# First four pairs of a chunked scan: products over 128 tokens, full-height tiles, and a new order of all pieces

## The chip, the cores and the metric

The kernel runs on one core of a Trainium2 chip. The metric is device microseconds of one execution, and the median of the runs is compared. One execution of each kernel is also profiled; its instructions, waits and transfers are what this text reads. TensorE (PE) multiplies, and its weight loads are listed apart as PEld. VectorE (DVE), ScalarE (ACT) and GpSimd (POOL) do the elementwise work, and SyncE (SP) issues the transfers.

## The reference

Two blocks follow each other. The first is a chunked scan (Mamba-2's SSD) over 4 batches, 8 heads and 768 tokens, with a head width of 32 and a state of 16:

```python
cum = np.cumsum(log_a[chunk])
M = (C @ B.T) * exp(cum[i] - cum[j]) * (i >= j)
y = M @ x + (C @ state) * exp(cum)
state = exp(sum) * state + sum_j exp(cum[-1] - cum[j]) * B[j] x[j]
```

The heads are then laid side by side to 256 channels (`x` below is that `y`), and a mixer follows:

```python
h = xt @ U @ V                      # xt: tokens last; rank 32
u = x + h.transpose(0, 2, 1)
out = u + np.maximum(u @ w_ch1, 0.0) @ w_ch2
```

with `w_ch1` of 256 x 1024 and `w_ch2` of 1024 x 256. U, V and both weights arrive as 64-bit floats and are turned into 32-bit ones on the chip.

## The kernel before, in words

**Pairs.** The scan takes 128 tokens as one block and two blocks as one pair, so there are 12 pairs, three for each batch. A block holds two chunks of 64 tokens. A pair is worked in steps, each named by a letter in the plan:

- `Q`, `P` (`prep`, L471): VectorE scales B and C by the decays F.
- `V`, `T` (`turning`, L483): TensorE transposes them, ScalarE copies the result to T and, masked by head parity, to Cm (a variant lets VectorE do Cm).
- `g` (`gram`, L518): C B^T. One product takes one head pair r (32 rows), one half p (64 columns) and one block c, with 128 moving columns: 16 products, in tiles of 32x64. Results lie in four PSUM banks.
- `m`, `M` (`mask`, L531): VectorE applies the causal mask to two of these banks each, 128x256 an operation, as a bitwise AND.
- `s` (`state`, L548) and `u` (`update`, L563): TensorE forms each chunk's addition to the state, VectorE runs the recurrence, POOL spreads the states by head (`Sm`, L585).
- `i`, `j` (`inter`, L615): C times the carried state, in two parts. Between the parts stands a guard on POOL (`apart`, L590, the copy at L592), which waits for the products before and holds up those behind.
- `n` (`intra`, L642): M x, 32 products, each over 64 rows (half p) and 32 columns, with 64 moving columns.
- `y` (`yout`, L657): ScalarE copies the result of one bank to yT; `t`, `O`, `o` turn it to tokens first (L671).

**Mixer.** For each batch: `p` (L694), `q` (L702) and `a` (L712) form h and add it to u. For batch 0, `U` are plain f32 products with `w_ch1` (L756, by the helper at L740), eight for each half of the tokens, and `d` the products with `w_ch2`. For the other batches the operands are split in parts first (`S`, `f`, `e`, `h`, `J`). All products of the mixer show under L740, all VectorE operations under L162, since a wrapper records them.

**Conversion.** `c` steps (`to_fp32`, L412) convert the weights, a block at a time: c1 is U and V together; c0 and c2 are the two halves of the first quarter of `w_ch1`; c3 to c5 are its other quarters (w1f); c6 to c9 are `w_ch2` (w2c). `R` refines them for the later batches. Work tiles come from a rotating set named words, of 15.

**Order.** Nothing is reordered by the compiler. `LOADS` and then `PLAN`, a string of words executed from left to right (`follow`, L875), fix the order in which every engine gets its instructions; each engine works its own queue in order. `A0`, `A1` (L371) make the decays F out of the logarithms; `K0` (L390) makes the chunk decays kept; `F` words are fills (L141), products of ones that keep TensorE occupied. Loads (`b`, `x`, `W`, `w`, `Z`, `z`, `B`, `X`, `L`) go into SP's queue in the order of the plan.

Of the kernel before, what the change touches and what calls it, by code (L numbers as in the profile page):

```python
# [10 lines left out]
FP32 = mybir.dt.float32  # L11
INT32 = mybir.dt.int32
# [20 lines left out]

LOADS = (
    'b0.0 b0.1 b0.2 x0.0 x0.1 b1.0 b1.1 b1.2 ')
PLAN = (
# [40 lines left out]


@with_exitstack
def kernel(  # L80
# [285 lines left out]
    for v in range(2):  # L366
        half = slice(v * H, v * H + H)
        vector.tensor_scalar(out=causal[half], in0=upto[half, half], scalar1=-1.0,
                                scalar2=None, op0=ALU.mult)

    def decays(bs, tag="w", which=range(2)):  # L371

# [98 lines left out]
    def prep(k, c=0, n=2):  # L471

        b, q = pairs[k]
        if "BC" not in st.setdefault(k, {}):
            st[k]["BC"] = att.tile([P, 2, 2, NH, N], FP32, tag="BC", name="BC", bufs=3)
        for g in [slice(4) if n == 2 else slice(c, c + 1) if c < 2 else slice(2, 4)]:
            part = st[k]["BC"].rearrange("p i c h n -> p (i c) h n")[:, g]
            vector.tensor_tensor(
                out=part, in0=bc_sb[k].rearrange("p h i c n -> p (i c) h n")[:, g],
                in1=F[:, b, q].rearrange("p h i c -> p (i c) h")[:, g, :, None].to_broadcast(  # L480
                    part.shape), op=ALU.mult)
# [32 lines left out]
    def four(tags, *dims):  # L514

        return [bank(tags[r], *dims) for r in range(4)]

    def gram(k, tags="xxzz"):  # L518
        s = st[k]
        s["g"] = g = four(tags, 2, 2, H)  # L520
        for c in range(2):
            for p in range(2):
                for r in range(4):
                    rows, cols = ts(r, Q), ts(p, H)
                    nc.tensor.matmul(  # L525
                        out=g[r][cols, c], lhsT=s["T"][rows, 0, c, cols],
                        rhs=s["Cm"][rows, :, :, ts(2 * c + p, Q)].rearrange("r v t i -> r v i t"),
                        start=(c == 0), stop=True,
                        skip_group_check=True)

    def mask(k, rows=range(4)):  # L531
        s = st[k]
        g = s["g"]
        if "M" not in s:
            s["M"] = att.tile([P, 4, 2, 2, H], FP32, tag="M", name="M")
        M = s["M"]
# [61 lines left out]
    def channels(k):  # L598

        s = st[k]  # L600
        if "y" not in s:
            s["y"] = [bank("y", 2, 2, H) for p in range(2)]
            s["seen"] = set()
        return s["y"]

# [9 lines left out]
    def inter(k, part):  # L615
# [3 lines left out]
        b, q = pairs[k]  # L619
        s = st[k]  # L620
        y = channels(k)
        after = [apart(k)] if part else []
        for c in range(2):
            for r in range(4):
                p = (part + r // 2) % 2
                own = st.get(("Sm", b, 4 * q + 2 * c + p))
                assert own is not None or 4 * q + 2 * c + p == 0
                if own is not None:
                    product = nc.tensor.matmul(  # L629
                        out=y[p][ts(r % 2, H), r // 2, c], lhsT=own[ts(r, Q)],  # L630
                        rhs=s["T"][ts(r, Q), 1, :, ts(2 * c + p, Q)].rearrange("r t i -> r i t"),
                        start=fresh(k, p, range(2 * (r % 2), 2 * (r % 2) + 2)),
                        stop=True, skip_group_check=True)
                    if part == 0:
                        behind.setdefault(k, []).append(product)
                    for op in after:
                        tc.add_manual_dep(
# [4 lines left out]
    def intra(k):  # L642

        s = st[k]
        y = channels(k)
        for n in range(2):
            for c in range(2):
                for p in range(2):
# [8 lines left out]
    def yout(k, p):  # L657
        b, q = pairs[k]
        if b not in yT:
            yT[b] = mix.tile([P, NCB, S], FP32, tag="yT", name="yT")  # L660
            ytok[b] = mix.tile([P, NC, DM], FP32, tag="ytok", name="ytok")
        yp = yT[b][:, :, ts(q, 2 * P)].rearrange("p g (c v i) -> p g c v i", c=2, v=2)
        nc.scalar.copy(out=yp[:, :, :, p], in_=st[k]["y"][p])  # L663

# [260 lines left out]
```

## Time and profile before

| | us |
|---|---|
| median of 3 runs | 220.32 |
| range of the runs | 219.8 to 224.22 |
| the profiled execution | 220.41 |
| its span, first to last instruction | 218.7 |
| TensorE busy | 210.3 |
| weight loads busy | 182.4 |
| VectorE busy | 154.0 |
| ScalarE busy | 114.2 |
| POOL busy | 17.7 |

The profiled execution's time is its span and 1.7 us around it. Matmuls are pipelined, so that a busy TensorE is not one at its peak; the busy time of weight loads separates the stages better. A timeline row has start, length, engine, line, operation, output and inputs, shapes and count, and in brackets the idle time before it and what ended it. A plain f32 product stands as two records.

### The profile page before, as it was taken

The numbers are of one execution on the slowest core, as the hardware profiler recorded it, in microseconds if no ns is written. First come the engines' busy times: TensorE is split into PE (matmuls) and PEld (weight loads), VectorE is DVE, ScalarE is ACT, GpSimd is POOL, SyncE is SP. The second block draws the span as 40 slices with busy tenths as digits, with TensorE's granted clock in tenths as the row PEclk, the third lists the DMA queues.
The fourth block names the chain that finished last, engine by engine and source line by source line (L and its number), as shares of the span: only waits on it lengthen the run. The fifth ranks groups of instructions, "written<-read, shape, count | busy, mean of one in ns | idle before, by whom it ended". The sixth has DMA issues, their size and how long they took to land.

```text
span 218.7 us, 6992 instructions
## 1 busy us (share of the span) xinstructions
PE 210.3 (96%) x2988; PEld 182.4 (83%) x2988; DVE 154.0 (70%) x330; ACT 114.2 (52%) x261; POOL 17.7 (8%) x41
## 2 busy tenths in 40 slices
PE   7999899999899999999999999999999999999993
PEld 4667566665677889998998999999999999999992
DVE  4687689999983996349796697566575945757813
ACT  3335967798357554645555458153565364466220
POOL 6021020010300210002120000100000000000000
PEclk9999999999999999999999999999999999999999
DMA  6986879896082170080000450100000010100003
GB/s 87 132 118 150 152 103 330 233 207 88 3 124 47 19 132 4 18 126 3 27 3 1 53 118 0 51 10 24 0 0 24 17 34 3 48 3 22 3 24 120
DMA packets 69519, 14.56 MB, mean 67 GB/s; under 512 B 63793, under 2 KB 67697, under 8 KB 69489
## 3 DMA queue, kind: packets, MB, share of 16 engines
q1 hardware_dynamic: 69488, 14.13, 32.5%
q8 instruction: 23, 0.38, 0.8%
q14 instruction: 8, 0.06, 0.1%
HBM read 10.98 MB, written 3.15 MB: 65 GB/s over the span
## 4 chain that ended last, share of the span: by engine, by line
PE 83%; DVE 11%; issue 2%; ACT 1%; DMA 1%; POOL 0%; DVEq 0%; POOLq 0%; ACTq 0%
PE x L740 27%; PE z L740 22%; PE y L740 12%; DVE words L162 5%; PE y L651 3%; PE y L629 3%; PE x L525 2%; PE w L671 2%; DVE M L162 2%; PE w L494 2%; DVE S L162 2%; PE w L557 1%; PE z L525 1%; PE w L694 1%; DMA a_sb<-in_a_dram 1%
## 5 line engine op out<-in xcount | busy, mean ns | idle before, releaser
L162 DVE SCALAR_TENSOR_TENSOR words<-words 128x768 fp32r<-128x768 f32 (+6 forms) x44 | 33.8, 799 | 0.3
L740 PE MATMUL x<-u,w 128*128 128x384 f32 x144 | 32.1, 342 | 0.0
L740 PE MATMUL z<-u,w 128*128 128x384 f32 x144 | 32.1, 342 | 0.0
L740 PEld LDWEIGHTS x<-u,w 128*128 128x128 f32 x144 | 24.6, 188 | 0.4 <-issue 0.2
L740 PEld LDWEIGHTS z<-u,w 128*128 128x128 f32 x144 | 24.3, 188 | 0.4 <-issue 0.2
L740 PE MATMUL x<-w2c,words 128*128 128x256 f32 x112 | 22.8, 339 | 0.7 <-DVE w2c L162 0.7
L745 ACT ACTIVATE x<-x 128x384 f32<-128x384 f32 (+1 forms) x30 | 13.6, 454 | 18.8 <-PE x L740 17.3
L745 ACT ACTIVATE z<-z 128x384 f32<-128x384 f32 (+1 forms) x27 | 12.5, 463 | 18.3 <-PE z L740 14.5
L740 PE MATMUL y<-w,words 128*128 128x256 f32 x144 | 20.3, 280 | 0.0
L740 PEld LDWEIGHTS x<-w2c,words 128*128 128x128 f32 x112 | 18.2, 189 | 2.4 <-DVE w2c L162 0.9
L162 DVE SCALAR_TENSOR_TENSOR words<-x,words 128x384 fp32r<-128x384 f32 x24 | 13.0, 552 | 9.7 <-ACT words L774 9.6
L740 PEld LDWEIGHTS y<-w,words 128*128 128x128 f32 x144 | 19.2, 188 | 0.0
L162 DVE SCALAR_TENSOR_TENSOR words<-z,words 128x384 fp32r<-128x384 f32 x24 | 12.8, 550 | 6.7 <-ACT words L774 6.7
L740 PE MATMUL x<-w,words 128*128 128x256 f32 x96 | 14.3, 285 | 0.0
L585 POOL TENSOR_TENSOR Sm<-S,own 128x256 f32<-128x256 f32 (+1 forms) x12 | 8.1, 676 | 76.3 <-DVE S L162 44.7
L774 ACT ACTIVATE words<-x 128x384 fp32r<-128x384 f32 x24 | 11.4, 488 | 5.6 <-PE x L740 5.6
L774 ACT ACTIVATE words<-z 128x384 fp32r<-128x384 f32 x24 | 11.3, 492 | 5.0 <-PE z L740 5.0
L162 DVE SCALAR_TENSOR_TENSOR S<-S,kept,w 128x64 f32<-128x64 f32 x40 | 11.2, 279 | 2.8 <-PE w L557 0.9
L740 PEld LDWEIGHTS x<-w,words 128*128 128x128 f32 x96 | 12.9, 189 | 0.1
L740 PE MATMUL z<-w2c,words 128*128 128x256 f32 x56 | 11.5, 339 | 0.2 <-DVE S L162 0.2
L651 PE MATMUL y<-M,x 64*32 64x64 f32 x768 | 10.5, 225 | 1.0 <-issue 0.9
L663 ACT COPY yT<-y 128x256 f32<-128x256 f32 x24 | 7.8, 380 | 6.9 <-PE y L629 6.9
(154 smaller groups left out, 400.0 us busy)
## 6 DMA issues: line engine op xcount, KB each, us to landing
words<-in_moe_w_ch_dram SPq DMA_DIRECT2D x7, 512.0 KB, 5.2
x<-in_x_dram SPq DMA_DIRECT2D x24, 128.0 KB, 3.4
out_dram<-ytok SPq DMA_DIRECT2D x24, 128.0 KB, 1.7
bc<-in_B_dram SPq DMA_DIRECT2D x24, 64.0 KB, 3.0
bc<-in_C_dram SPq DMA_DIRECT2D x12, 128.0 KB, 3.2
words<-in_moe_w_ch_dram SPq DMA_DIRECT2D x2, 256.0 KB, 3.7
words<-in_moe_V_dram SPq DMA_DIRECT2D x4, 48.0 KB, 1.9
words<-in_moe_U_dram SPq DMA_DIRECT2D x1, 192.0 KB, 4.0
```

The source lines that it names most:

```text
L162: self.last = call(*args, **kwargs)
L494: nc.tensor.transpose(out=tp[:, i, v], in_=s["BC"][:, i, c + v].rearrange("p h n -> p (h n)"), identity=ident)
L525: nc.tensor.matmul(out=g[r][cols, c], lhsT=s["T"][rows, 0, c, cols], rhs=s["Cm"][rows, :, :, ts(2 * c + p, Q)].rearrange("r v t i -> r v i ...
L557: nc.tensor.matmul(out=s["A"][p][ts(r, Q), v], lhsT=s["BC"][half, 0, v, 2 * r:2 * r + 2].rearrange("p h n -> p (h n)"), rhs=x_sb[k][half, ...
L585: nc.gpsimd.tensor_tensor(out=s["Sm"][:, sl], in0=s["S"][:, sl].rearrange("p i (s d) -> p i s d", s=2), in1=own2[:, b, 4 * q:4 * q + sl.st ...
L629: product = nc.tensor.matmul(out=y[p][ts(r % 2, H), r // 2, c], lhsT=own[ts(r, Q)], rhs=s["T"][ts(r, Q), 1, :, ts(2 * c + p, Q)].rearrange ...
L651: product = nc.tensor.matmul(out=y[p][ts(i, Q), n, c], lhsT=x_sb[k][half, c, h], rhs=s["M"][half, h // 2, c, h % 2], start=fresh(k, p, [i] ...
L663: nc.scalar.copy(out=yp[:, :, :, p], in_=st[k]["y"][p])
L671: nc.tensor.transpose(out=t[:, c, g], in_=yT[b][:, g, ts(2 * q + c, P)], identity=ident)
L740: nc.tensor.matmul(out=t, lhsT=lhsT, rhs=rhs, start=start, stop=True, skip_group_check=True)
L745: nc.scalar.activation(t, t, AF.Copy, scale=1.0 + EPS)
L774: nc.scalar.activation(gs[j, m // 2][0][:, m % 2], t, AF.Relu, scale=NEAR)
```

## The change

It applies to the first four pairs (`LIGHT`): the three of batch 0 and the first of batch 1.

- `gram`: one product for a head pair and a block over all 128 tokens, 256 moving columns: 8 products in tiles of 32x128.
- `mask`: the mask is `lower`, with the causal triangle in the two diagonal 64x64 blocks and zero elsewhere, made in the setup on POOL. An operation covers 128x512. Its output goes to two tiles of the words set in place of the M tile.
- `intra`: M x with all 128 rows and 128 moving columns, 16 products in tiles of 128x32.
- `inter`: the bank is chosen by head pair and not by chunk, and the guard on POOL is left out.
- `yout`: the copy writes 256 adjacent elements.
- `prep`: pairs 2 and 3 (`SCALED`) are scaled on POOL and not on VectorE.
- `PLAN`: all pieces and loads of the whole kernel stand in another order. At the beginning, V's loads (`Z0`) stand ahead of pair 2's, K0 and three fills ahead of A0, and pair 1's state behind its masks; pair 4's C B^T stands behind the first plain product. `LOADS` is the same.

```diff
+LIGHT = range(0, 4)
+SCALED = (2, 3)
 PLAN = (
-    'x1.1 F2.0 A0 Q0.1 x1.0 Q0.0 b2.2 A1 F2.1 Q0.2 V0.1.1 V0.0.0 K0 F3.3 Q1.2 Q1.1 g0 m0 Q1.0 s0 '
-    'V1.1.2 M0 n0 u0.0 u0.1 V1.0.2 b3.0 F2.1 Q2.1 s1 u1.0 u1.1 i0 g1 m1 F3.0 M1 b2.0 Q2.0 b2.1 Q2.2 '
...
-    'c0 o2 F2.3 v0 x4.1 b4.1 b4.2 u3.0 u3.1 p0 c2 n3 c0 P4 c0 i3 q0 c2 b5.2 b5.0 T4 T4 j3 y3.0 y3.1 '
-    'W2 W3 b5.1 W4 a0.0 c2 c2 a0.1 x4.0 w5 c3 c3 c3 X5 g4 c4 w8 c3 t3 w6 U0.0.0 m4 c4 U0.0.1 P5 c4 '
...
+    'x1.1 F2.0 Z0 K0 b2.2 F2.3 F2.1 F1.0 A0 A1 Q0.1 b2.1 Q0.0 b2.0 Q1.0 x1.0 x2.0 Q0.2 x2.1 b3.1 '
+    'b3.2 s0 V0.0.0 F2.1 u0.0 u0.1 V0.1.1 F3.3 b3.0 z0 Q1.2 g0 W0 Q2.2 Q2.1 V1.0.2 x3.0 F3.0 Q1.1 '
+    'V1.1.2 Q2.0 x3.1 b4.2 i0 M0 m0 g1 m1 M1 b4.1 n0 V2.1.3 j0 y0.1 b4.0 W2 s1 W1 V2.0.2 y0.0 u1.0 '
+    'n1 s2 W3 W4 u1.1 u2.0 u2.1 w6 g2 b5.1 m2 M2 i1 j1 y1.0 i2 y1.1 O0.0 t1 n2 c1 c1 x4.0 P3 j2 y2.0 '
+    'c1 y2.1 b5.0 w8 c0 T3 T3 O2.1 c0 s3 c1 g3 u3.0 c0 w5 u3.1 o2 m3 p0 i3 v0 M3 c0 P4 q0 n3 j3 c3 '
+    'y3.1 a0.1 T4 T4 a0.0 b5.2 c3 y3.0 c2 U0.1.0 c3 c3 g4 c5 t3 c2 U0.0.0 M4 c2 c5 c5 U0.1.3 c4 X5 '
...
+    lower = const.tile([P, 2, H], INT32)
+    nc.gpsimd.memset(lower, 0)
+    for v in range(2):
+        half = slice(v * H, v * H + H)
+        nc.gpsimd.tensor_copy(out=lower[half, v], in_=causal[half])
...
-            vector.tensor_tensor(
+            (nc.gpsimd if k in SCALED else vector).tensor_tensor(
...
+        if k in LIGHT:
+            s["g"] = g = four(tags, 2, 2, P)
+            for c in range(2):
+                for r in range(4):
+                    nc.tensor.matmul(
+                        out=g[r][:, c], lhsT=s["T"][ts(r, Q), 0, c],
+                        rhs=s["Cm"][ts(r, Q), :, :, ts(c, H)].rearrange("r v t i -> r v i t"),
+                        start=(c == 0), stop=True, skip_group_check=True)
+            return
...
+        if k in LIGHT:
+            t = raw.tile([P, 2 * WCOLS], INT32, tag="words", name="words", bufs=NWORDS)
+            M = t.rearrange("p (r c s i) -> p r c s i", r=2, c=2, s=2)
+            s.setdefault("Ms", {})[rows[0] // 2] = M.bitcast(FP32)
+            for r in rows:
+                vector.tensor_tensor(
+                    out=M[:, r % 2].rearrange("p c s i -> p (c s) i"),
+                    in0=g[r].bitcast(INT32).rearrange("p c s i -> p (c s) i"),
+                    in1=lower.rearrange("p v i -> p (v i)")[:, None, :].to_broadcast([P, 4, P]),
+                    op=ALU.bitwise_and)
+            return
...
-            s["y"] = [bank("y", 2, 2, H) for p in range(2)]
+            s["y"] = [bank("y", 2, P) if k in LIGHT else bank("y", 2, 2, H) for p in range(2)]
...
-        after = [apart(k)] if part else []
+        light = k in LIGHT
+        after = [apart(k)] if part and not light else []
...
+                    at = r // 2 if light else p
                     product = nc.tensor.matmul(
-                        out=y[p][ts(r % 2, H), r // 2, c], lhsT=own[ts(r, Q)],
+                        out=y[at][ts(r % 2, H), c, ts(p, H)] if light else
+                        y[p][ts(r % 2, H), r // 2, c], lhsT=own[ts(r, Q)],
...
+        if k in LIGHT:
+            for n in range(2):
+                for c in range(2):
+                    for i in range(4):
+                        nc.tensor.matmul(
+                            out=y[n][ts(i, Q), c], lhsT=x_sb[k][:, c, 4 * n + i],
+                            rhs=s["Ms"][n][:, i // 2, c, i % 2], start=fresh(k, n, [i]),
+                            stop=True, skip_group_check=True)
+            return
...
+        if k in LIGHT:
+            nc.scalar.copy(out=yT[b][:, p, ts(q, 2 * P)],
+                           in_=st[k]["y"][p].rearrange("p c i -> p (c i)"))
+            return
```

More of the change, by code (lines that the diff above doesn't have):

```diff
@@ L628, in inter @@
                 if own is not None:
+                    at = r // 2 if light else p
                     product = nc.tensor.matmul(
-                        out=y[p][ts(r % 2, H), r // 2, c], lhsT=own[ts(r, Q)],
+                        out=y[at][ts(r % 2, H), c, ts(p, H)] if light else
+                        y[p][ts(r % 2, H), r // 2, c], lhsT=own[ts(r, Q)],
                         rhs=s["T"][ts(r, Q), 1, :, ts(2 * c + p, Q)].rearrange("r t i -> r i t"),
-                        start=fresh(k, p, range(2 * (r % 2), 2 * (r % 2) + 2)),
+                        start=fresh(k, at, range(2 * (r % 2), 2 * (r % 2) + 2)),
                         stop=True, skip_group_check=True)
-                    if part == 0:
+                    if part == 0 and not light:
                         behind.setdefault(k, []).append(product)
```

70 rows, old and new, of the table PLAN are left out of this document.

## The prediction, made before the changed kernel ran

> **What bounds the kernel now.** I read the page first: the busy shares, the forty slices, the chain by engine.
>
> ```profile
> PE 210.3 (96%) x2988; PEld 182.4 (83%) x2988; DVE 154.0 (70%) x330; ACT 114.2 (52%) x261; POOL 17.7 (8%) x41
> PEld 4667566665677889998998999999999999999992
> DVE  4687689999983996349796697566575945757813
> PE 83%; DVE 11%; issue 2%; ACT 1%; DMA 1%; POOL 0%; DVEq 0%; POOLq 0%; ACTq 0%
> ```
>
> Over the whole span TensorE bounds. The weight loads (PEld) separate two stages: 4 to 7 tenths in the first twelve slices, 9 from the middle on. VectorE is densest in slices 7 to 12. So I cut the span with the windows view (columns: stretch, its length, then busy time and instructions of PE, PEld, DVE, ACT, POOL, then clock and DMA).
>
> ```profile
> 5.93:33.83 27.90, 25.43 (x716) 17.93 (x720) 21.54 (x65) 15.91 (x46) 4.12 (x9) 1.00 0.83 139
> 34.81:60.00 25.19, 24.48 (x248) 15.54 (x246) 24.34 (x54) 17.88 (x36) 3.49 (x3) 1.00 0.67 158
> 80.00:203.50 123.50, 123.50 (x1520) 118.47 (x1505) 83.38 (x152) 63.50 (x144) 4.67 (x10) 1.00 0.12 28
> ```
>
> From 80 us TensorE is full and does only work that the change leaves alone. What the change can move is how late the full stage begins. Two queues decide that: until 34 us VectorE works 21.54 of 27.90 us (6.36 idle); from 35 to 60 us VectorE is full (24.34 of 25.19) with the weight conversion while TensorE does the plain products of batch 0. The chain in order of time shows both.
>
> ```profile
> 35.08 1.29 PE x L740 x4
> 50.54 2.50 DVE words L162 x4
> 59.30 0.61 DVE w2c L162
> 59.95 1.25 PE x L740 x5
> 65.41 0.87 PE z L740 x4
> ```
>
> The first line is two plain f32 products of 384 columns, in 4 records: 1.29 us, 0.84 ns a column and record. The next three show the conversion on VectorE and TensorE taking up again when the last converted block (w2c) is there, at 59.9. The last is one down piece of batch 0 (four records of 256 columns): 0.87 us.
>
> **Part 1: the products themselves.** Timeline rows:
>
> ```profile
> 28.58 0.86 PE L694 MATMUL x<-ytok,UV 128*32 128x256 f32 x16
> 29.37 0.86 PE L651 MATMUL y<-M,x 64*32 64x64 f32 x64
> 30.16 0.49 PE L629 MATMUL y<-T,Sm 32*64 32x64 f32 x12
> 33.45 0.35 PE L525 MATMUL x<-Cm,T 32*64 32x128 f32 x2 [0.16 <-ACT Cm L504]
> 34.19 0.30 PE L525 MATMUL z<-Cm,T 32*64 32x128 f32 x2
> 34.43 0.66 PE L671 MATMUL w<-ident,yT 128*128 128x128 f32 x4
> 34.92 0.49 PE L740 MATMUL x<-yT,w1f 128*128 128x384 f32 x1
> ```
>
> M x for a pair is 64 records of 64 columns, 29.37 to 30.16: 0.79 us. One after another at 0.84 ns they would take 3.44 us, so 4.4 of 8 tiles run at a time. After, it is 32 records of 128 columns: again 3.44 us in a row, in four tiles. The nearest row with 128x32 tiles is the projection L694: 8 records of 256 and 8 of 128 columns, 2.58 us in a row, took 0.79 (28.58 to 29.37), 3.3 at a time. So 0.86 (four at a time) to 1.05 us. C B^T is 32 records of 128 columns now (first and last quoted, 0.74 us of starts in that pair), 16 of 256 after: the same 0.86 to 1.05. TensorE pays 0.2 to 0.6 us more a pair, 0.7 to 2.3 us for four. All of it lies before 34 us, where TensorE waits for VectorE; I count none there, except that masks begin later after C B^T (0.35 us, for two of four, below). Uncovered, it is the 2.3 us. The guard on POOL between the two inter-chunk halves (L592) goes for four pairs. Its row stands in the next fence: 0.487 us each, and the waits shown are POOL's own. I count nothing, and put a gain of at most 4 x 0.49 us into the range. The copies to yT keep their 256 elements: nothing.
>
> **Part 2: VectorE up to the first plain product.** Groups by form (busy, mean ns of one):
>
> ```profile
> L162 DVE TENSOR_TENSOR M<-x,causal 128x256 int32<-128x256 int32 x24 | 9.0, 417 | 0.6 <-PE z L525 0.5
> L162 DVE TENSOR_TENSOR yT<-x,yT 128x384 f32<-128x384 f32 x8 | 4.4, 552 | 2.4 <-PE x L712 2.4
> L162 DVE TENSOR_TENSOR BC<-bc,F 128x512 f32<-128x512 f32 x9 | 6.2, 684 | 0.5 <-issue 0.5
> L162 DVE TENSOR_TENSOR BC<-bc,F 128x128 f32<-128x128 f32 x6 | 1.6, 285 | 1.0 <-ACT F L386 1.0
> L162 DVE TENSOR_TENSOR BC<-bc,F 128x256 f32<-128x256 f32 x3 | 1.3, 421 | 0.4 <-ACT F L386 0.4
> L162 DVE TENSOR_SCALAR words<-words 128x256 int32<-128x256 int32 x4 | 1.4, 396 | 0.0
> L162 DVE TENSOR_SCALAR words<-words 128x512 int32<-128x512 int32 x14 | 6.1, 476 | 0.0
> L585 POOL TENSOR_TENSOR Sm<-S,own 128x256 f32<-128x256 f32 x8 | 6.0, 745 | 40.1 <-DVE S L162 36.0 <-PE z L740 4.1
> L592 POOL COPY settled<-slot 128x1 f32<-128x1 f32 x12 | 5.8, 487 | 48.7 <-PE y L629 37.5 <-PE y L651 11.1
> ```
>
> Sixteen masks grow from 256 to 512 elements. 256 to 384 elements is 417 to 552 ns, so 512 is about 0.683: 16 x 0.266 = +4.26 us. The scalings of pairs 2 and 3 go to POOL: 2 x 0.285 + 0.421 + 0.684 = -1.67. Reordering puts two conversion steps of 256 behind (-0.79) and two of 512 ahead (+0.95); the two operations of the chunk decays (below) leave this stretch, -1.05. Counted in the program's order, the operations from the first scaling to the additions that release the first plain product sum to 24.65 us of durations before and 26.26 after. Before, 24.65 occupied 21.54 us, so 26.26 occupies 23.0: +1.5 us.
>
> **Part 3: the start.** K0 (chunk decays, L394, L397) and three fills (L141) now stand ahead of A0 (L379) in TensorE's queue.
>
> ```profile
> 4.64 0.87 PE L379 MATMUL w<-la,ref 128*128 128x192 f32 x2
> 7.75 0.49 PE L394 MATMUL z<-la,middle 128*128 128x192 f32 x2
> 8.62 0.81 PE L141 MATMUL y<-one 128*128 128x384 f32 x2
> 12.84 0.60 PE L141 MATMUL x<-one 128*128 128x256 f32 x2
> 5.93 0.49 DVE L162 TENSOR_TENSOR BC<-bc,F 128x128 f32<-128x128 f32 x2 [1.02 <-ACT F L386]
> 6.78 0.42 DVE L162 TENSOR_TENSOR BC<-bc,F 128x256 f32<-128x256 f32 x1 [0.36 <-ACT F L386]
> 7.73 0.61 DVE L162 TENSOR_SCALAR Cm<-w,slot 128x128 f32<-128x128 f32 x2 [0.53 <-PE w L494]
> 8.82 0.53 DVE L162 TENSOR_TENSOR words<-z,mine 128x352 f32<-128x352 f32 x1 [0.48 <-PE z L397]
> 9.38 0.52 DVE L162 TENSOR_REDUCE kept<-words 128x44 f32<-128x352 f32 x1
> 23.65 0.63 DVE L162 TENSOR_SCALAR words<-words 128x384 int32<-128x384 int32 x2 [1.21 <-DMA words<-in_moe_U_dram]
> ```
>
> K0 took 0.87 us of starts (7.75 to 8.62). The fills are 640 columns in two records, 1.08 us at 0.84 ns. That is 2.0 us, and up to 3.9 if records run half as fast, as L379 does near 4.6 us (0.87 for two of 192 columns). I take 2.9, in between, as the array warms on the way. VectorE's first scaling goes from 5.93 to 8.8. VectorE does the decays in that wait. Of its 6.36 us of idle time the first pieces (0.36, 0.53, 0.48) then have no cause, and neither has the 1.21 us for U, whose load stays at about the same place in SP's queue while its conversion comes later; twice 0.35 us come with the longer C B^T: 4.5 us. The V loads now stand ahead of pair 2's loads and of half of x of pair 1 on SP; pair 1's state is also needed later, so nothing, and the range covers 1 us. POOL's scaling of pair 3 has 512 elements, 1.4 us at 745 ns for 256, against 0.68 on VectorE; masked by VectorE's queue, in the range too.
>
> **The sum.** 8.8 + 23.0 + 4.5 = 36.3 us for the additions that ended at 33.83 (33.28 and 0.55 long): +2.5 us. Before, C B^T of pair 4 and transposes stood ahead of the first plain product (33.45 to 34.92); now behind it, and the waits inside go, which leaves TensorE 2.8 us later at equal work. From there to 60 us TensorE idled 0.7 us (25.19 - 24.48), which its larger backlog fills. The profiled execution took 220.41 us (span 218.7, 1.7 around it; the median of the runs, 220.32, is the same within 0.1). 220.4 + 2.8 - 0.7 = 222.5 us.
>
> The Trainium skill, "TensorEngine Tiling (Array Packing)", Key Properties, says that changing the tiling mode drains TensorE. C B^T and the inter-chunk product shared one shape and no longer do. An estimate by that rule: two more switches in each of four pairs, each one record's 0.22 us, is 1.8 us, which would make 224.3; the row L629 starts 0.79 us after L651 and does not separate a drain, so no run here shows it yet.
>
> **Rivals.** (a) *Slower: conversion decides.* From those additions to the last converted block VectorE has 29.3 us of durations before and 31.9 after. Before it took 26.1 us (33.8 to 59.9), so after 28.4, ending at 64.7. TensorE has about 30 us of work ahead of the first product that needs the block (15 plain products at 1.29, four down pieces at 0.87, some 7.5 us of C B^T, M x, states and transposes of pairs 4 to 6), which lasts to about 66.5. For it: the cover is thin, and the chain ran on VectorE until 59.9. If the cover is not there because those products wait for masks and earlier blocks, the whole lateness of the conversion, 64.7 - 59.9 = 4.8 us, counts: 225.2. It decides as soon as VectorE loses 2 us more than counted. (b) *Shorter chain.* Four independent pairs, states first and no guard, leave VectorE 1 us of idle time instead of 4.5, and the start costs 2.0: 222.5 - 3.5 - 0.9 = 218.1, with the guard's 2 us also gained 216. Against it: nothing shows the guard on the path. (c) *The tiles do not overlap four at a time:* 3.44 us instead of 0.86 for 8 products, +20 us, of which at most 6 are covered: over 230; L694 speaks against it. (d) *Issue bounds the products.* If M x's 64 records were bound by their number, half of them would halve 0.79 us, for C B^T likewise: 3 us less, 219.5. The Trainium skill, "TensorE: Matmul & The Clock Gate", section "Wait — 56ns, not 53.3ns?", states a floor of about 25 ns from start to start. The trace disagrees: 64 records in 0.79 us are 12 ns apart.
>
> **How the numbers follow.** Chances: forecast 0.54, (a) 0.18, (b) 0.22, (c) 0.03, (d) 0.03. The forecast's own range is 220 to 224.5. 2% of 220.4 is 4.4 us, about what a measurement of this kernel can tell from no change: below 216.0 faster, above 224.8 slower. Faster: half of (b), 0.11. Slower: (a) and (c), 0.21. Within: 0.68. The range runs from (b) without the guard, less half a microsecond of lost idle time in the late stage, to (a) with 1.8 us of the uncounted product cost of 2.3: 217.5 to 227.0.
>
> **What would show it.** First scaling at 8.8 us, not 6; masks of 512 elements at 0.68 us; M x and C B^T of a pair at 0.9 to 1.05 us; the additions done at 36.3; the last w2c at 64.7 with no TensorE wait for it. A first scaling before 7.5, or a TensorE wait of 2 us or more near 60, makes the forecast wrong, on either side.

## The result and the profile after

The changed kernel takes 221.72 us in the median of 9 runs (221.42 to 222.71), the kernel before 220.56 on the same chip (219.12 to 224.22). The ratio is 1.0078, 95% interval 1.0054 to 1.0102: slower by 0.8%, or 1.2 to 2.2 us, and within the 2% that the text before calls no change. The profiled executions are 221.42 and 220.41 us, 1.0 apart. (One kernel below, the order alone, was disturbed in four of its six executions, the profiled one among them; its ratio rests on the other two, 227.1 and 228.0 us.)

The page of the changed kernel, busy shares and the chain by engine:

```profile
PE 211.9 (96%) x2796; PEld 182.4 (83%) x2796; DVE 155.9 (71%) x326; ACT 114.0 (52%) x261; POOL 17.5 (8%) x44
PE 88%; DVE 5%; ACT 3%; issue 1%; DMA 1%; DVEq 0%; ACTq 0%
```

VectorE's share of the chain fell from 11% to 5%, TensorE's rose from 83% to 88%: the kernel is a little slower although the wait at the conversion is gone. The stretches, cut at the first scaling, the additions and 60 us (length, then busy time of PE, PEld, DVE, ACT, POOL, clock, DMA):

```profile
7.78:35.40 27.62, 24.72 (x495) 16.58 (x494) 23.27 (x59) 14.31 (x42) 4.89 (x9) 1.00 0.91 184
35.40:60.00 24.60, 24.36 (x287) 15.01 (x286) 23.74 (x56) 20.68 (x42) 1.60 (x3) 1.00 0.60 120
60.00:80.00 20.00, 20.00 (x422) 16.21 (x422) 10.77 (x28) 8.23 (x19) 1.60 (x4) 1.00 0.50 78
```

VectorE works 23.27 of 27.62 us up to the additions; from 35.40 on TensorE is idle for 0.24 us and from 60 to 80 us not at all. The rows that answer the predicted steps, the start and VectorE's first (the masks as groups, with mean ns), then TensorE's:

```profile
4.68 0.72 PE L401 MATMUL z<-la,middle 128*128 128x192 f32 x2
6.88 0.49 PE L386 MATMUL w<-la,ref 128*128 128x192 f32 x2
7.78 1.03 DVE L164 TENSOR_TENSOR BC<-bc,F 128x128 f32<-128x128 f32 x4 [0.72 <-ACT F L393]
L164 DVE TENSOR_TENSOR words<-x,lower 128x512 int32<-128x512 int32 x8 | 5.1, 685 | 1.8 <-PE z L531 1.7
L164 DVE TENSOR_TENSOR words<-z,lower 128x512 int32<-128x512 int32 x8 | 5.1, 683 | 0.9 <-PE z L531 0.9
34.85 0.55 DVE L164 TENSOR_TENSOR yT<-z,yT 128x384 f32<-128x384 f32 x1
64.53 0.69 DVE L164 SCALAR_TENSOR_TENSOR w2c<-words 128x512 f32<-128x512 f32 x1
...
10.77 0.53 PE L531 MATMUL x<-Cm,T 32*128 32x256 f32 x2 [0.27 <-DVE Cm L164]
11.70 0.44 PE L531 MATMUL z<-Cm,T 32*128 32x256 f32 x2
12.07 0.44 PE L501 MATMUL x<-ident,BC 128*128 128x128 f32 x2
18.21 1.08 PE L680 MATMUL y<-words,x 128*32 128x128 f32 x32
19.27 0.32 PE L584 MATMUL w<-x,BC 64*32 64x64 f32 x8
34.99 1.56 PE L783 MATMUL x<-yT,w1f 128*128 128x384 f32 x4
```

K0 begins at 4.68, A0 at 6.88, and the first scaling is at 7.78. Masks take 0.68 us each, and what VectorE waits for ahead of them is C B^T (1.7 and 0.9 us). C B^T of the first pair lasts 1.30 us from its first start to the next product's (10.77 to 12.07), M x 1.06 (18.21 to 19.27). The additions end at 35.40, against 33.83 before. The last w2c is converted at 64.53 to 65.22, and no row of TensorE waits for it.

### The profile page after: what moved, and what is told of

Read it like the earlier page. It is cut to its first block, busy times and chain, and to the rows that moved or that the text cites. A ratio compares the mean times of both kernels' runs of the same rounds, so it can differ in the third digit from the quotient of the medians.

```text
span 219.7 us, 6607 instructions
## 1 busy us (share of the span) xinstructions
PE 211.9 (96%) x2796; PEld 182.4 (83%) x2796; DVE 155.9 (71%) x326; ACT 114.0 (52%) x261; POOL 17.5 (8%) x44
## 4 chain that ended last, share of the span: by engine, by line
PE 88%; DVE 5%; ACT 3%; issue 1%; DMA 1%; DVEq 0%; ACTq 0%
PE x L783 31%; PE z L783 23%; PE y L783 12%; PE y L658 3%; PE y L690 2%; PE w L501 2%; PE x L531 2%; PE w L714 2%; DVE words L164 2%; PE x L541 1%; PE w L584 1%; DVE S L164 1%; PE w L737 1%; ACT Cm L511 1%; PE z L541 1%
## 5 line engine op out<-in xcount | busy, mean ns | idle before, releaser
L783 PEld LDWEIGHTS z<-u,w 128*128 128x128 f32 x144 | 24.8, 188 | 0.1
L783 PE MATMUL y<-w,words 128*128 128x256 f32 x144 | 19.5, 280 | 0.0
L783 PEld LDWEIGHTS y<-w,words 128*128 128x128 f32 x144 | 18.5, 188 | 0.2 <-ACT z L788 0.2
L783 PE MATMUL x<-w,words 128*128 128x256 f32 x96 | 13.7, 282 | 0.0
L783 PE MATMUL x<-yT,w1f 128*128 128x384 f32 x32 | 11.4, 489 | 0.0
L505 ACT COPY T<-w 128x512 f32<-128x512 f32 (+1 forms) x10 | 5.7, 568 | 10.3 <-PE w L501 10.3
```

Source lines behind the costliest of these rows:

```text
L505: nc.scalar.copy(out=s["T"][:, :, c:c + n], in_=tp)
L783: nc.tensor.matmul(out=t, lhsT=lhsT, rhs=rhs, start=start, stop=True, skip_group_check=True)
```

## The experiments

Prices are stated against the kernel before, as ratios with intervals; 0.1% is 0.22 us. The changed kernel's own ratio, 1.0078, is what most of them are held against.

**1. The order alone.** `LIGHT` and `SCALED` empty, so that only `PLAN` differs from before in the pairs.

```diff
-LIGHT = range(0, 4)
-SCALED = (2, 3)
+LIGHT = range(0)
+SCALED = ()
```

> The order of after with the products, masks, copies and scalings of before for all twelve pairs. Theory (VectorE's stretch up to the additions sets the end; the large masks and the late start are what the new order has to make up for): sixteen masks are 0.266 us shorter (-4.26), two pairs' scalings come back to VectorE (+1.67), so the additions come about 2.6 us earlier than 35.4, near 33, and the time is 221.7 - 2.6 = 219.1, or 1.0 more where C B^T for 64 columns does not help: 218.5 to 220. Rival A (the order of the loads and late pieces is what costs the 1.2 us, products and masks lie under other work): no change against after, 221.7. Rival B (the new order only fits independent products; the guard and the dependent halves stall in it): slower than after, 222.5 to 224.

Measured: ratio 1.0335 (1.0281 to 1.0389), 7.4 us slower than before. The theory had it at 219, and it fails: without the large masks this kernel is slower than both, and beyond rival B's 224 too. VectorE's rows, from the stretch of 5.88 to 16.12 us, in which the granted clock of its profiled execution was 1.0:

```profile
13.46 0.83 DVE L164 TENSOR_TENSOR BC<-bc,F 128x256 f32<-128x256 f32 x3 [1.94 <-DMA bc<-in_C_dram]
14.97 0.29 DVE L164 TENSOR_TENSOR BC<-bc,F 128x128 f32<-128x128 f32 x1 [0.69 <-DMA bc<-in_B_dram]
```

Two scalings of pair 2, at the head of VectorE's queue, wait 1.94 and 0.69 us for loads of C and B, and everything behind them waits too. That is a part of the 7.4 us; experiment 7 finds another.

**2. The products alone.** The new products, masks and copies in the order of before, all scalings on VectorE; the guard of the light pairs is left out here too.

```diff
-SCALED = (2, 3)
+SCALED = ()
-PLAN = ( ... the new order
+PLAN = ( ... the order of before
```

> The order of before with the light products, masks and copies for the first four pairs, all scalings on VectorE. Theory: VectorE gets 4.26 us more before the additions, nothing is taken off it, the guard is gone, C B^T takes 1.3 us a pair and not 0.74; of VectorE's 6.36 us of idle time in that stretch at most about 1.5 can take it up: 220.5 + 3 to 5 = 223.5 to 225.5, first plain product at 38 to 40 us. Rival A (masks lie in VectorE's idle time, the order costs): 220.5 to 221.5. Rival B (the guard and the two-part products were on the path and make up for the masks): below 220.5.

Measured: 226.76 us, ratio 1.0301 (1.0267 to 1.0334). The additions end at 39.66:

```profile
39.11 0.55 DVE L164 TENSOR_TENSOR yT<-z,yT 128x384 f32<-128x384 f32 x1
```

That is 5.8 us later than before, of which the sixteen masks are 4.26. This fits the theory in kind, with the masks on the path, and the time is about 1.3 us above its range. Two other things are in it. TensorE stops for 0.88 us at 154.69, a kind of stop that experiment 7 finds. And the granted clock of this execution was 0.5 from 32.50 to 35.91 us, which is in the 5.8; three executions at a clock of 1.0 took 226.58 to 227.51 us all the same. So either half of the change measures 3% slower, and both together 0.8%.

**3. The scalings back on VectorE.**

```diff
-SCALED = (2, 3)
+SCALED = ()
```

> After, with the scalings of pairs 2 and 3 on VectorE again. Theory (VectorE before the additions is the path): +1.67 us there less what its remaining 4.3 us of idle time takes up, so 222.3 to 223.4, additions done at 36 to 37. Rival (POOL's slower scalings were late for their pairs, so the move bought nothing): 221.0 to 221.9.

Measured: 223.72 us, ratio 1.0167 (1.0131 to 1.0203), 0.9% or 2.0 us above the changed kernel. Two rows of VectorE, and POOL's scaling of 512 elements in the changed kernel:

```profile
13.28 1.03 DVE L164 TENSOR_TENSOR BC<-bc,F 128x256 f32<-128x256 f32 x4 [1.99 <-DMA bc<-in_C_dram]
37.04 0.55 DVE L164 TENSOR_TENSOR yT<-z,yT 128x384 f32<-128x384 f32 x1
```

```profile
L485 POOL TENSOR_TENSOR BC<-bc,F 128x512 f32<-128x512 f32 x1 | 1.1, 1107 | 0.0
```

The additions end at 37.59, 2.2 us later. It is not only the 1.67 us of work: the scaling of pair 2 waits 1.99 us for its load, ahead of the masks in the same queue. On POOL a wait for a load holds up nothing on VectorE, though 512 elements take 1.1 us there. A part of the 2.0 is the clock: in the profiled execution it was 0.5 from 15.80 to 19.21 us, and the three executions at 0.988 to 0.990 took 224.06 to 224.84 us; the three at 0.996 to 1.0 took 223.11 to 223.37, 1.4 above the changed kernel.

**4. The decays ahead of the chunk decays,** as they stood before.

```diff
-F2.0 Z0 K0 b2.2 F2.3 F2.1 F1.0 A0 A1 Q0.1 b2.1 Q0.0 b2.0 Q1.0 x1.0 x2.0 Q0.2
+F2.0 Z0 A0 b2.2 A1 Q0.1 b2.1 Q0.0 b2.0 Q1.0 x1.0 x2.0 Q0.2 K0 F2.3 F2.1 F1.0
```

> After, with the decays A0 A1 ahead of the chunk decays K0 and of the three fills, and K0's VectorE work behind the first scalings, as it stood before. Nothing is left out. Theory (the late start costs what it delays): first scaling at 5.9 instead of 7.78 (-1.85), the two operations for the chunk decays come back into the stretch (+1.05), pieces of idle time too: 221.7 - 0.8 = 220.9, additions at 34.6. Rival A (the start has slack because transfers or TensorE set the additions): unchanged, 221.7, with VectorE idle longer further down. Rival B (early fills and K0 are needed for what follows): slower, 222.5.

Measured: 222.35 us, ratio 1.0103 (1.0071 to 1.0135): no gain, and rather 0.5 us more than the changed kernel, though the intervals overlap.

```profile
5.92 0.49 DVE L164 TENSOR_TENSOR BC<-bc,F 128x128 f32<-128x128 f32 x2 [1.09 <-ACT F L393]
7.70 0.63 DVE L164 TENSOR_TENSOR BC<-bc,F 128x128 f32<-128x128 f32 x2 [1.28 <-DMA bc<-in_B_dram]
8.24 0.52 DVE L164 TENSOR_TENSOR words<-z,mine 128x352 f32<-128x352 f32 x1
35.31 0.55 DVE L164 TENSOR_TENSOR yT<-z,yT 128x384 f32<-128x384 f32 x1
```

The first scaling is back at 5.92, but the third, of pair 1, waits until 7.70 for its load of B. In the changed kernel VectorE does the chunk decays in that time, and here they come behind (8.24 to 9.31): the additions end at 35.86, 0.46 later. The late start was nearly free, and undoing it is not.

**5. Without the three fills** ahead of A0.

```diff
-K0 b2.2 F2.3 F2.1 F1.0 A0 A1
+K0 b2.2 A0 A1
```

> After without the three fills between the chunk decays K0 and the decays A0. Only products of ones are left out. Theory (a late start costs little, because pair 1's B lands at 7.7 and its scaling is third in VectorE's queue): first scaling at 6.7 instead of 7.78, third at 7.7 instead of 8.19, so 0.4 to 0.5 us less: 221.3. Rival A (the fills' 1.08 us count in full): 220.7. Rival B (the fills keep the array ready, the first products become slower): 221.7 or more.

Measured: 221.78 us, ratio 1.0105 (1.0067 to 1.0143): nothing gained. ScalarE's and VectorE's rows:

```profile
7.18 0.24 ACT L413 ACTIVATE kept<-kept 128x44 f32<-128x44 f32 x1 [2.69 <-DVE kept L164]
7.32 0.55 ACT L393 ACTIVATE F<-w 128x192 f32<-128x192 f32 x2
7.68 0.37 DVE L164 TENSOR_TENSOR BC<-bc,F 128x128 f32<-128x128 f32 x1 [0.53 <-ACT F L393]
```

A0 is 1 us earlier, and the first scaling still at 7.68. ScalarE works its queue in order, and K0's exponential (L413) stands ahead of that of the decays F (L393): it waits for VectorE's reduction, which ends at 7.14. So the fills were covered, and neither the prediction nor the expectation had looked at ScalarE's queue.

**6. The guard put back** for the light pairs.

```diff
-after = [apart(k)] if part and not light else []
+after = [apart(k)] if part else []
-if part == 0 and not light:
+if part == 0:
```

> After, with the guard on POOL between the two inter-chunk halves put back for the four light pairs. Theory (it lies beside other work, as the prediction counted): 221.7, at most 0.3 more. Rival (its 0.49 us a pair and the wait for M x lie on the path): 222.7 to 223.7.

Measured: 223.50 us, ratio 1.0181 (1.0134 to 1.0227), 1.0% or 2.3 us above the changed kernel. The time is the rival's, but not all of it is shown to be the guard's. The profiled execution was the longest of six (224.79): its first scaling came 0.6 later, its granted clock was 0.5 from 23.47 to 26.88 us (0.83 from 20 to 30), and TensorE stopped for 0.75 us at 57.47, inside one group of M x, as in experiment 7. Its rows around the guard:

```profile
23.37 0.87 PE L658 MATMUL y<-T,Sm 32*64 32x64 f32 x24 [0.41 <-POOL settled L619]
24.06 0.65 ACT L702 COPY yT<-y 128x256 f32<-128x256 f32 x2 [2.92 <-PE y L658]
27.48 1.06 DVE L164 SCALAR_TENSOR_TENSOR words<-words 128x384 f32<-128x384 f32 x2 [2.15 <-ACT words L437]
```

TensorE waits 0.41 us for the guard, ScalarE copies that pair's result at 24.06 instead of 22.69 (0.6 of it from the start), and the conversion of U and V behind that copy keeps VectorE idle for 2.15 us (0.52 in the changed kernel). Of that increase about 0.9 us goes with the clock: the two groups of transposes ahead of the conversion take 1.90 us of starts here and 1.03 in the changed kernel. At a clock of 1.0 four executions took 221.99 to 223.63, with a middle of 223.3, 1.6 above the changed kernel, or 2.1 when each is held against the kernel before that ran beside it. How much of that is the guard and how much a stop like the one at 57.47 isn't separated; the wait of 0.41 us is what is seen of the guard itself.

**7. The order alone, with POOL's scalings:** experiment 1 with `SCALED = (2, 3)`.

> The order of after with the products, masks and copies of before for all pairs, but the scalings of pairs 2 and 3 on POOL as in after. Theory (the order alone lost because scalings that wait for loads stood in VectorE's queue): the waits of 1.9 and 0.7 us for the loads of B and C and 1.67 us of scalings go, which gives 227.1 - 4.3 = 222.8, and the smaller masks bring it below after, 219.5 to 221. Rival (the new order stalls on the guard and on the dependent halves of the old products): 224 to 227, and waits of VectorE for the states and of TensorE around the guard stay.

Measured: 227.27 us, ratio 1.0319 (1.0263 to 1.0375). Up to the additions the theory is right: no load is waited for, and they end at 34.82, 0.6 before the changed kernel's. Then the time is lost again, in places that no one had counted: TensorE stops at 104.28, 146.44 and 156.72 us for 1.33, 1.04 and 0.76 us, and at 18.36, ahead of the additions, for 0.99. A row of each kind, the second from the kernel before (it has one such piece, at 22.59):

```profile
103.95 0.33 PE L584 MATMUL w<-x,BC 64*32 64x64 f32 x11
105.61 0.42 PE L584 MATMUL w<-x,BC 64*32 64x64 f32 x21 [1.33 <-issue]
```

```profile
22.05 0.54 PE L651 MATMUL y<-M,x 64*32 64x64 f32 x34
23.50 0.45 PE L651 MATMUL y<-M,x 64*32 64x64 f32 x30 [0.91 <-issue]
```

In both, TensorE stands still in the middle of one group of equal products, and the releaser is "issue": it waits for nothing that the profile shows. The four pieces are 4.12 us against 0.91 in the kernel before, 3.2 of the 4.4 us between the two profiled executions (224.79 and 220.41).

**8. C B^T in 32x64 tiles,** each product of the light pairs split in two column halves.

```diff
-for r in range(4):
-    nc.tensor.matmul(out=g[r][:, c], lhsT=s["T"][ts(r, Q), 0, c],
+for p in range(2):
+    for r in range(4):
+        nc.tensor.matmul(out=g[r][ts(p, H), c], lhsT=s["T"][ts(r, Q), 0, c, ts(p, H)],
```

> After, with C B^T of the light pairs in tiles of 32x64, eight at a time: each product is split in two column halves, the same multiplications and the same results, 32 records of 256 columns instead of 16. Theory (four tiles of 32x128 start a group only every 0.27 us because the next weights load late; the 0.55 us more per pair are on the path through the masks): with eight tiles 0.9 to 1.0 us a pair and not 1.3, three waits of VectorE 0.3 shorter: 220.7 to 221.2. Rival (the pace is set by the moving data of a row group, which two column halves do not share): twice the records take 1.7 us or more, 222.5 to 223.5.

Measured: 227.62 us, ratio 1.0366 (1.0316 to 1.0417), and both reasons given for it are wrong. VectorE does not see the edit: the additions end at 35.50, 0.10 later. C B^T takes what it took:

```profile
10.80 0.48 PE L532 MATMUL x<-Cm,T 32*64 32x256 f32 x2 [0.27 <-DVE Cm L164]
11.09 0.47 PE L532 MATMUL x<-Cm,T 32*64 32x256 f32 x2
12.07 0.44 PE L501 MATMUL x<-ident,BC 128*128 128x128 f32 x2
...
63.08 0.64 PE L659 MATMUL y<-T,Sm 32*64 32x64 f32 x24 [0.70 <-issue]
106.99 0.41 PE L585 MATMUL w<-x,BC 64*32 64x64 f32 x20 [1.33 <-issue]
149.40 0.29 PE L542 MATMUL x<-Cm,T 32*64 32x128 f32 x1 [1.51 <-issue]
159.38 0.41 PE L784 MATMUL x<-w,words 128*128 128x256 f32 x2 [0.59 <-issue]
```

Eight tiles start a group of eight every 0.27 to 0.29 us, as four started a group of four: 1.27 us for the pair, against 1.30. The loss is the last four rows: 0.70 + 1.33 + 1.51 + 0.59 = 4.13 us of "issue", long after the light pairs are done. With the 0.10 that is 4.2 of the 5.1 us between the two profiled executions.

A theory for these pieces: the page lists a queue named instruction.

```profile
q8 instruction: 22, 0.36, 0.7%
```

22 transfers, in the trace 16,384 bytes each, go with 2796 products and as many weight loads: 5592 / 22 = 254 to a transfer, 64 bytes each. In the trace of the split tiles one begins at 104.79 and ends at 105.75, and TensorE goes on at 106.99; for the others it begins at 60.62, 146.52 and 157.02. Each time TensorE goes on 2.2 to 2.9 us after the transfer's start. In the changed kernel one begins at 104.50, and from 105.8 on TensorE is in products of 384 columns, which need few instructions. So it should matter where in the stream of small products a transfer's boundary falls, and any change in the number of TensorE's instructions moves all later boundaries. Three kernels put that to the test.

**9. The changed kernel, shifted.** Nothing of its work is changed; 32 tiny products replace two thirds of the first fill, in the time in which TensorE waits for its first input.

```diff
-warm(3, "x")
+small = bank("x", 4 * P)
+idle(small, 1)
+for i in range(32):
+    part = slice(i % 4 * Q, i % 4 * Q + Q)
+    nc.tensor.matmul(out=small[part, P + 8 * i:P + 8 * i + 8],
+                     lhsT=one[part].to_broadcast([Q, Q]), rhs=one[part].to_broadcast([Q, 8]), ...
```

> After, with 32 tiny products (32x32 tiles, 8 columns) in place of two thirds of the very first fill, in the time in which TensorE waits for its first input. Everything behind them is unchanged; they only shift TensorE's stream of instructions by 128, counted as two records and two weight loads a product, which is half of one 16 KB transfer of the queue named instruction at 64 bytes each (22 transfers for 5657 records and loads). Theory (where these transfers fall against the dense groups of small products decides the idle pieces put down to issue): the late idle pieces of the version with C B^T in 32x64 tiles, 0.7, 1.3, 1.5 and 0.6 us at about 62, 106, 148 and 159 us, appear here too, though no product of the pairs is changed: 225 to 226.5. Rival (those pieces belong to the products in 32x64 tiles): 221.3 to 222.2, no idle piece.

Measured: 226.85 us, ratio 1.0300 (1.0266 to 1.0334), 2.2% above the changed kernel.

```profile
107.58 0.42 PE L591 MATMUL w<-x,BC 64*32 64x64 f32 x21 [1.29 <-issue]
149.46 0.34 PE L548 MATMUL x<-Cm,T 32*64 32x128 f32 x2 [1.04 <-issue]
159.18 0.62 PE L790 MATMUL x<-w,words 128*128 128x256 f32 x4 [0.49 <-issue]
36.12 0.55 DVE L164 TENSOR_TENSOR yT<-z,yT 128x384 f32<-128x384 f32 x1
PE 87%; DVE 5%; ACT 3%; issue 3%; DMA 1%; DVEq 0%; ACTq 0%
```

Three of the four pieces are there, at the places named, 2.82 us together; "issue" rises from 1% to 3% of the chain. The tiny products also delayed the start: the additions end at 36.67, 1.27 later. With 0.41 us of TensorE's idle time between 60 and 80 us that is 4.5 of the 5.0 us between the profiled executions.

**10. The 32x64 tiles, shifted,** by the same edit.

> The version with C B^T in 32x64 tiles, with the same 32 tiny products ahead. It has 32 products more than after in the light pairs, 128 instructions, so with the tiny ones 256, one whole transfer: theory: the idle pieces at 62, 106, 148 and 159 us go, C B^T takes what it took, 221.7 to 222.5. Rival (they belong to those products): 227 to 228, pieces stay.

Measured: 223.27 us, ratio 1.0136 (1.0110 to 1.0162), 2.3% less than without the tiny products, though they add work. The four pieces are gone, and one of 0.68 us has come at 55.60. The additions end at 36.15, 0.75 later than the changed kernel's; 0.75 + 0.68 is 1.4 of the 1.7 us to its profiled execution. One shift brings the pieces to a kernel that had none, and takes them from one that had four. That they come from TensorE's instruction transfers is shown by these two and by a count over all fourteen traces. Behind 8 us these have 24 pieces of "issue" over 0.25 us on TensorE. Counted among TensorE's records (products, weight loads and the sequencer's own), each of the 24 falls at the same place: 193 records and a multiple of 256 stand ahead of it. Each ends 1.2 to 1.6 us after a transfer has ended. The 0.91 us of the kernel before is one of them.

**11. The order alone with POOL's scalings, shifted,** by the same edit.

> The order alone with scalings on POOL, with the same 32 tiny products ahead. Against after that version has 96 products more, 384 instructions, and with the tiny ones 512, two whole transfers. Theory: the three late idle pieces (1.3, 1.0 and 0.8 us) go, 227.3 - 3.1 = 224.2 or less, down to 222; what stays above after is lost before 35 us in the waits of the old products. Rival: 227, the pieces stay.

Measured: 227.96 us, ratio 1.0328 (1.0294 to 1.0363): the time did not fall. The three late pieces are gone, as expected (after 80 us TensorE is idle for 0.14 us), and others have come early:

```profile
19.37 0.69 PE L697 MATMUL y<-M,x 64*32 64x64 f32 x44 [1.17 <-issue]
22.13 0.48 PE L665 MATMUL y<-T,Sm 32*64 32x64 f32 x11 [0.84 <-POOL settled L626]
24.40 0.90 PE L665 MATMUL y<-T,Sm 32*64 32x64 f32 x20 [1.78 <-issue]
PEclk9999659999999999999999999999999999999999
```

1.17 and 1.78 us of "issue" inside M x and the inter-chunk product, and 0.84 for the guard between them; the additions end at 40.32 instead of 34.82. Not all of these 5.5 us are the stops: the last line, from the page, is the granted clock in 40 slices of 5.65 us, in tenths, and it fell to 0.5 from 23.94 to 34.18 us, right behind them. Whether the stops brought the clock down was not tested. A further stop of 0.63 us stands at 59.86. So a shift moves the pieces, it does not remove them.

**12. Before, with POOL's scalings** and nothing else of the change.

> Before, with nothing of the change but the scalings of pairs 2 and 3 on POOL. TensorE's order is untouched. Theory (VectorE's work ahead of the additions of batch 0, and ahead of the last converted block, is the path in before): 1.67 us less there, a part of it lost as waits, 220.2 - 0.7 to 1.5 = 218.7 to 219.5, additions near 32.5. Rival (POOL takes 1.1 us for 512 elements and has the guards and the spreading of states to do, so pairs 2 and 3 or their guards come late): 220.2 to 221.5.

Measured: 220.47 us, ratio 1.0013 (0.9984 to 1.0043): no difference. VectorE's rows:

```profile
17.97 0.61 DVE L162 TENSOR_SCALAR Cm<-x,slot 128x128 f32<-128x128 f32 x2 [1.48 <-PE x L494]
20.12 0.92 DVE L162 SCALAR_TENSOR_TENSOR S<-S,kept,w 128x64 f32<-128x64 f32 x3 [1.55 <-POOL settled L592]
25.36 0.76 DVE L162 TENSOR_TENSOR M<-z,causal 128x256 int32<-128x256 int32 x2 [2.05 <-PE z L525]
```

VectorE's 1.67 us went, and waits of 1.48, 1.55 (for the guard) and 2.05 us (for C B^T) stand there (0.64, 0.11 and 0.49 at the same places before). The time is the rival's, but the guard is only the second of these waits. Ahead of the third TensorE stopped for 1.15 us ("issue", 22.94 to 24.09) inside M x, right before that C B^T; the kernel before has its 0.91 there. VectorE's work was not what set these rows. No kernel of this study is faster than the one before.

## Why the prediction came out, point by point

*The sum.* Predicted 222.5 us, the forecast of a small loss. The profiled execution is 221.42. The gap of 1.1 is nearly all one term, the start; but other terms came out by luck.

*The start* was put at 2.9 us, between 2.0 and 3.9. It is 1.85 (5.93 to 7.78): K0 and the fills took 2.2 us (4.68 to 6.88), near the lower bound. And the reason was wrong: experiment 5 shows that the fills cost nothing, because ScalarE does K0's exponential ahead of the decays F. Nor is the 1.85 a loss of that size: by experiment 4 only about 0.5 us of it could be had back, and the chunk decays would then cost 1.05.

*VectorE's stretch* was right in its totals. 23.0 us busy was predicted and 23.27 measured, 4.5 idle and 4.35 measured. The masks took 0.685 and 0.683 for the predicted 0.683. But the idle time is made of other pieces than those counted. The waits for C B^T grew from 0.6 to 2.6 us where 0.7 more had been counted, and all other waits together fell from 5.8 to 1.7, about 1.5 more than counted. The two errors cancel, and that is luck. The additions come 1.57 us later instead of 2.5, nearly all of the difference from the start (1.85 for 2.9). That the masks are on the path, experiment 2 supports.

*C B^T and M x.* M x took 1.06 us for a predicted 0.86 to 1.05. C B^T took 1.30, above its upper end of 1.05: a mis-sized term. Its groups of four records of 256 columns start every 0.27 us, where 0.84 ns a column makes 0.215; the first takes 0.35. VectorE waits for it three times, the 2.6 us in the groups shown above.

*The guard* was counted as nothing, with a gain of "at most 4 x 0.49 us" for the range. That was probably too little: in experiment 6 the kernel with the guard is 2.3 us slower by the ratios (interval 1.0134 to 1.0227 against 1.0054 to 1.0102), 1.6 to 2.1 at a clock of 1.0. But a stop of 0.75 us at an instruction transfer is in at least one of these executions, so the guard's own price stays open. The row in the prediction showed only POOL's own waits; who stands behind the guard, TensorE's second half and ScalarE's copy, it did not show.

*The scalings on POOL* were worth 1.67 us in the sum and are worth 1.4 at a clock near 1.0 and 2.0 over all executions in this order (experiment 3), since a load that is late then stops only POOL. In the order of before they are worth nothing (12).

*The late stage.* The last w2c was predicted to be done at 64.7; it begins at 64.53 and ends at 65.22, though the additions came 0.9 earlier than predicted, so VectorE's way from the one to the other took 29.8 us for 28.4. TensorE still does not wait for it. Rival (a) is out, and so is (c): the tiles overlap. The 0.70 us that TensorE waited at 59.25 before is gone, as the 0.7 in the sum said: 1.57 - 0.7 is 0.9 of the 1.0 us between the profiled executions. Rival (b), the shorter chain, had the cheap start right and is still not what came, since VectorE kept 4.35 us of idle time, 2.6 of it for C B^T. Rival (d) is not what happened either: half as many records did not make the products shorter.

*The tiling mode.* From the rule in the Trainium skill, "TensorEngine Tiling (Array Packing)", Key Properties, that a change of tiling mode drains TensorE, the prediction had worked out an estimate of 1.8 us, and 224.3. The terms above leave no room for it, and experiment 8, where C B^T has the inter-chunk product's tile shape again, has the same additions within 0.10 us and 1.27 us for C B^T against 1.30.

*What the prediction had no term for* is the instruction transfers. The changed kernel has 192 records fewer (2796 for 2988), so all later boundaries moved, and behind 8 us it has no piece of "issue" above 0.3 us, where before had one of 0.91. By experiment 9 the same work could have come out 3 us slower; that the forecast has no such term and is still near is luck. As an estimate, the profiled executions less their stops are 219.5 us before (220.41 - 0.91) and 221.4 after, so the placing of the boundaries may hide as much as a second 0.9 us of loss. The Trainium skill, "Runtime: NRT & Kernel Launch", Instruction fetch mechanics, states blocks of 16 KiB or 256 instructions and that crossing a boundary is mostly hidden. The traces agree with the size (254 records and loads to a transfer, and the 24 pieces 256 records apart or a multiple of it). They agree with the rest for most crossings, and for all behind 8 us in the changed kernel, but not where small products are dense: 0.49 to 2.37 us at a crossing.

*What stays open.* The order alone with POOL's scalings has a median 2.5 us above its profiled execution (227.27 and 224.79); four of its five other executions had a granted clock of 0.990 to 0.992, against 1.0 in the profiled one, but they left no trace, so where they lose time isn't known. The guard's own price is not separated from stops and clock. And how a plan could be chosen so that no boundary falls in a dense group was not tried.

## What to carry to other kernels

Price a wait or a guard not by its own row but by the queues behind it, and a moved step in every queue that it issues to: here ScalarE's order hid three fills, and a late load that was free on POOL held up VectorE's queue for 2 us. Compare an idle time piece by piece with the one predicted, since errors can cancel in its total. Any change in the number of TensorE's instructions shifts where its instruction transfers fall, and among dense small products that brought stops of 2.8 us (experiment 9) and 4.1 us (8), 1.3 and 1.9% of the time; look for idle time put down to "issue" inside one group of equal products before you explain a difference by the edit itself, and shift the stream by some tiny products to tell. Look at the granted clock of every execution, too. Each half of this change alone measured 3% slower and both together 0.8%, and it is tempting to conclude that the layout and the order need each other. That is not shown: as an estimate, the order with POOL's scalings (7) less its stops is at 220.7 us (224.79 - 4.12), below the changed kernel's 221.4.

## What the runs showed of the hardware

At some of its 16 KB instruction transfers TensorE stopped: 24 stops of 0.49 to 2.37 us in the fourteen traces, each with 193 of its records and a multiple of 256 ahead of it, each ending 1.2 to 1.6 us after a transfer had. In 15 of them the 256 records ahead had gone by in 1.3 to 2.1 us; apart from four, all stretches of 256 without a stop took 3.0 us or more. A shift of the stream by half a transfer brought and removed these stops. The granted clock fell to 0.5 for 3.4 us in experiments 2, 3 and 6 (from 32.50, 15.80 and 23.47 us) and for 10.2 us in 11 (from 23.94), always in the stage before 36 us; in the changed kernel's nine executions it was 1.0. Products of 256 columns over 32 rows started a step every 0.27 us, with four tiles of 32x128 and with eight of 32x64 alike. GpSimd's scaling of 128x512 took 1.1 us (VectorE 0.68), where 1.4 had been estimated.
